# A fused layernorm, window attention and gated projection on one core: group scaling issued later, V copies on two engines, one load and the last rows rearranged

## The chip, the core and the metric

The kernel runs on one core of a Trainium2 chip. A core has a matrix engine (TensorE, PE in the profile; its weight loads are shown as PEld), a vector engine (VectorE, DVE), an activation engine (ScalarE, ACT), a general engine (GpSimd, POOL), and a queue processor (SyncE, SP) that here only issues DMAs. Each engine works through its own list of instructions in order and waits on semaphores for the others. Matmul results go to PSUM, which has eight banks of 128 x 512 fp32; everything else lies in SBUF or, outside, in DRAM. The metric is the time of one execution on the device in microseconds; lower is better.

## What is computed

```python
x  = A_x                                   # 1 x 2048 x 640, bf16
xn = (x - mean) / sqrt(var + 1e-5)
# A: attention, 32 heads of 20, causal window of 256 rows
q, k, v = split(xn @ wqkv)                 # 640 x 1920
scores = (q @ k.T) * 20 ** -0.5            # masked: 0 <= i - j < 256
o = softmax(scores) @ v
# B: gated projection
h = sigmoid(xn @ w_gate) * (xn @ w_up)     # 640 x 1536 each
return x + o @ wo + h @ w_down
```

## The kernel before

The 2048 rows are cut into four chunks `c` of 512, and a chunk into four slices `s` of 128 rows. A chunk passes these stages:

- `g_norms`: mean and variance on DVE (`bn_stats`, `bn_aggr`), `rstd` on POOL (`rstd_block`), then `xn` on DVE (`norm_block`); a DMA transpose on SP (`turn_block`) gives `xnT`. Chunk 0 is transposed on PE.
- `g_qk`: five blocks of q and five of k, each of 5 matmuls of 512 columns (`proj_block`, L297). Each block is cast to bf16 in a tile `st` (q on DVE L301, k on ACT L303), stored to a DRAM scratch (L305) and read back in another layout by `spread` (L312). The pool of `st` has five buffers; the warm-up at the start used the first one.
- `g_v`: V of each slice in two halves of 5 matmuls with 320 columns (`project_v` L323), copied to the tile `v` by `copy_v` (L330), on DVE by default.
- `g_gu`: gate and up projections, 12 blocks each of 5 matmuls (`pg` L395, `pu` L402). ACT makes `th` = tanh(pg/2) (L398, one buffer), DVE makes `h` = (th + 1) * pu (L406).
- `g_out`: for each slice, `down` accumulates 12 matmuls per half of 320 columns (L415), `outp` adds 5 matmuls with `wo` (L428), then DVE adds x (`add_half`, L433), and SP stores the rows (L448). The factor 2 of `h` is undone by the scale 0.5 there.

The attention of a chunk runs beside this in steps. A step has the score matmuls (L465, to one tile `ps` of four banks), two exponentials on ACT (L471), and maskings on POOL (L475). When the steps of a group of four heads are done, `pv` (L496) multiplies by V into the bank `acc`, and `finish_group` has DVE transpose `acc` to the tile `t1` (L506, one buffer), take the reciprocal of the sums (L508), scale the pieces (L512), and transpose a full set back to `oc` (L516). `oc` is read by the `wo` matmuls of that chunk's output.

Two things set the order. Each engine gets its instructions in the order in which the Python code issues them. The dense stages are generators in a list (`Fill`); a loop over the attention steps issues one step, and pulls dense pieces up to the share of work that belongs to it. So a dense piece of 5 to 6 matmuls is the unit between two attention steps. Before a step, `pv` of a group that ended two steps earlier is issued, with its `finish_group`.

The pool `ps_d` has three PSUM banks in turn for all dense results (pqk, pv, pg, pu, y), `acc` has one, `ps` four. At the end the `ps` banks are returned, and all four slices of the last chunk do `down` first (with the last group's `pv` after slice 1), each half in a bank of its own, then all do `outp`. The last slice stores its two halves separately, the first from ACT's queue and the second from SP's.

At the start SP issues, in this order: rows of chunk 0 and the V part of `wqkv`, the q and k parts, the first halves of `w_gate` and `w_up`, the x rows of chunk 1 (`load_x(1)`, 640 KB), and `clear` twice (zeros into the padding of the scratch, 384 KB each); then come the stores of q and k blocks as these are made.

Of the kernel before, what the change touches and what calls it, by code (L numbers as in the profile page):

```python
# [9 lines left out]
P = 128  # L10
S = 2048
D = 640
# [3 lines left out]
DC = D // P  # L16
FC = F // P
CW = 512
NCH = S // CW
SBC = CW // P  # L20
HG = 4
NG = H // HG
GH = NG // 2
VW = DH + 1
HALF = 320
# [4 lines left out]
ADD = mybir.AluOpType.add  # L30
MULT = mybir.AluOpType.mult
# [3 lines left out]
BF16 = mybir.dt.bfloat16  # L35
FP32 = mybir.dt.float32
# [75 lines left out]
def kernel(  # L112
# [11 lines left out]
    nc = tc.nc  # L124
    x2 = A_x.flatten_outer_dims()
    out2 = out.flatten_outer_dims()
# [7 lines left out]
    lnp = pool("lnp", 4)  # L134
# [11 lines left out]
    ps_a = pool("ps_a", 1, space=bass.MemoryType.PSUM)  # L146
    ps_d = pool("ps_d", 3, space=bass.MemoryType.PSUM)
# [6 lines left out]
    xc = {}  # L154

    def load_x(c):
        t = xp.tile([P, SBC, D], BF16, name="xc")
        xc[c] = t
        nc.sync.dma_start(out=t, in_=xr[:, c * SBC:(c + 1) * SBC, :])
# [5 lines left out]
    wd = const.tile([P, FC, D], BF16, name="wd")  # L165
# [33 lines left out]
            nc.sync.dma_start(out=t[k], in_=w.rearrange("(c p) f -> p c f", p=P)[:, :, k * FS:(k + 1) * FS])  # L199

    load_gu(0)
    load_x(1)
    clear("q", 0)
    clear("k", 0)

# [84 lines left out]
    def proj_block(w, c, m):  # L290


        base = 0 if w == "q" else D
        ps = ps_d.tile([P, CW], FP32, name="pqk", tag="d")
        for d in range(DC):
            wt = wqkv[:, d, base:base + D].rearrange("p (k m) -> p m k", m=DC)
            nc.tensor.matmul(ps, lhsT=wt[:, m, :], rhs=xnT[c][:, d, :],  # L297
                             start=(d == 0), stop=(d == DC - 1))
        st = stp.tile([P, CW], BF16, name="st")
        if w == "q":  # L300
            nc.vector.tensor_copy(out=st, in_=ps)  # L301
        else:
            nc.scalar.copy(out=st, in_=ps)  # L303
        dst = scratch[w, c % 2].rearrange("(h j) s -> h j s", j=32)
        nc.sync.dma_start(out=dst[:, 4 * m:4 * m + 4, :], in_=st)  # L305
# [27 lines left out]
    def proj_v(c, s, hf, copy=nc.vector.tensor_copy):  # L333
        copy_v(c, s, hf, project_v(c, s, hf), copy)
# [26 lines left out]
    def g_qk(c):  # L361
        for w in "qk":
            for m in range(DC):
                proj_block(w, c, m)
                if w == "k" and m == 1:
                    spread("q", c, 0, NG if c else 2)
                yield 5 * MM
        if c == 0:
            spread("k", c, 0, 1)
            spread("k", c, 1, 3)  # L370
            spread("q", c, 2, 4)
            spread("k", c, 3, 4)

    def g_v(c):
        for s in range(SBC):
            new_v(c, s)
            for hf in range(2):
                proj_v(c, s, hf)
            if s == 0:
                spread("k", c, 0, 2)  # L380
                spread("k", c, 2, NG)
            yield 10 * 136
# [26 lines left out]

    oc = {}  # L410

    def down(c, s, ys):
        for hf in range(2):
            for f in range(FC):
                nc.tensor.matmul(ys[hf], lhsT=ht[c, f][:, s * P:(s + 1) * P],  # L415
                                 rhs=wd[:, f, hf * HALF:(hf + 1) * HALF],
                                 start=(f == 0), stop=False)
                if f == 5:
                    yield 6 * 136
            yield 6 * 136  # L420

    def outp(c, s, ys, last=False):
        sb = c * SBC + s
        y = lnp.tile([P, D], BF16, name="xn", bufs=5)

        def wo_half(hf):
            for m in range(DC):
                nc.tensor.matmul(ys[hf], lhsT=oc[c, m][:, s * P:(s + 1) * P],  # L428
                                 rhs=wo[:, m, hf * HALF:(hf + 1) * HALF],
                                 start=False, stop=(m == DC - 1))  # L430

        def add_half(hf):
            nc.vector.scalar_tensor_tensor(  # L433
                out=y[:, hf * HALF:(hf + 1) * HALF], in0=ys[hf], scalar=0.5,
                in1=xc[c][:, s, hf * HALF:(hf + 1) * HALF], op0=MULT, op1=ADD)

        if last:
            for hf in range(2):
                wo_half(hf)
                add_half(hf)  # L440
                cut = slice(hf * HALF, (hf + 1) * HALF)
                (nc.scalar, nc.sync)[hf].dma_start(out=out2[sb * P:(sb + 1) * P, cut], in_=y[:, cut])
        else:
            wo_half(0)
            wo_half(1)
            add_half(0)
            add_half(1)
            nc.sync.dma_start(out=out2[sb * P:(sb + 1) * P, :], in_=y)  # L448
        yield 10 * 136

    def g_out(c):
        for s in range(SBC):
            ys = [ps_d.tile([P, CW], FP32, name=f"y{i}", tag="d")[:, 0:HALF] for i in range(2)]
            yield from down(c, s, ys)
            yield from outp(c, s, ys)


    def scores(c, step):
# [30 lines left out]
    def pv(c, g, parts):  # L489
        acc = ps_a.tile([P, CW], FP32, name="acc")  # L490
        flat = [(pt, *piece[1:]) for step, pt in parts for piece in step["pv"] if piece[0] == g]
        for k, (pt, r, q, n, col) in enumerate(flat):
            v = vt[c * SBC + r]
            for i in range(HG):
                h = g * HG + i
                nc.tensor.matmul(  # L496
                    acc[32 * i:32 * i + 32, q * U:(q + n) * U],
                    lhsT=v[:, h * VW:h * VW + 32], rhs=pt[:, i, col * U:(col + n) * U],
                    start=(k == 0), stop=(k == len(flat) - 1), skip_group_check=True)
        finish_group(c, g, acc)  # L500
# [3 lines left out]
    def finish_group(c, g, acc):  # L504
        t1 = np_.tile([P, 16, 32], FP32, name="t1")
        nc.vector.transpose(out=t1.rearrange("p b r -> p (b r)"), in_=acc)  # L506
        rec = np_.tile([P, 16, 1], FP32, name="rec")
        nc.vector.reciprocal(rec, t1[:, :, DH:VW])  # L508
        for m, slot, first, n in pieces_of(g):
            if slot == 0:  # L510
                on[m] = onp.tile([P, 16, 32], BF16, name="on")
            nc.vector.tensor_tensor(out=on[m][:, :, slot:slot + n], in0=t1[:, :, first:first + n],  # L512
                                    in1=rec.to_broadcast([P, 16, n]), op=MULT)
            if slot + n == 32:
                oc[c, m] = op.tile([P, CW], BF16, name="oc")
                nc.vector.transpose(out=oc[c, m], in_=on[m].rearrange("p b r -> p (b r)"))  # L516


    class Fill:
        def __init__(self):  # L520
            self.parts = []
            self.done = set()
            self.shut = set()

# [8 lines left out]
        def one(self):  # L533
            label, gen, _ = self.parts[0]
            try:
                cost = next(gen)
                self.parts[0][2] -= cost
                return cost
            except StopIteration:
                self.parts.pop(0)  # L540
                self.done.add(label)
                return 0

        def pull(self, ns):
            while ns > 0 and self.parts and self.parts[0][0] not in self.shut:
# [118 lines left out]
    for t, (c, k, step) in enumerate(todo):  # L664
        if k == 0 and c > 0:
            fill.until(f"qk{c}")
        if k == 2 and c > 0:
            fill.until(f"v{c}")
        for group in [x for x in ends if ends[x] == t - 2]:
            pv(*group, parts.pop(group))  # L670
            if group[1] == NG - 1:
                fill.shut.discard(f"out{group[0]}")
        made = (step, scores(c, step))
        for g in dict.fromkeys(piece[0] for piece in step["pv"]):
            parts.setdefault((c, g), []).append(made)
        last, label = next(x for x in cuts if t < x[0])
        credit += fill.left(label) * step["units"] / sum(x[2]["units"] for x in todo[t:last])
        credit = fill.pull(credit)
    fill.pull(10 ** 9)

    c = NCH - 1

    def run(gen):
        for _ in gen:
            pass

    banks.close()
    ps_y = pool("ps_y", 2 * (SBC - 1) - 2, space=bass.MemoryType.PSUM)
    homes = [(ps_y, "y")] * 4 + [(ps_d, "d")] * 3 + [(ps_a, "acc")]
    tiles = [lambda p=p, n=n: p.tile([P, CW], FP32, name=n)[:, 0:HALF] for p, n in homes]  # L690
    ys = [None] * SBC
    for s in range(SBC):
        ys[s] = [tiles[2 * s](), tiles[2 * s + 1]()]
        run(down(c, s, ys[s]))
        if s == 1:
            pv(c, NG - 1, parts.pop((c, NG - 1)))
    for s in range(SBC):
        run(outp(c, s, ys[s], s == SBC - 1))
# [1 line left out]
_INS = ['A_x', 'A_wqkv', 'A_wo', 'B_x', 'B_w_gate', 'B_w_up', 'B_w_down']  # L700
_OUTS = [((1, 2048, 640), 'bfloat16')]
# [25 lines left out]
```

The softmax here doesn't subtract the row's maximum and nothing guards it: scores larger than these inputs give would overflow.

## Time and profile before

| what | value |
|---|---|
| time, median of 8 runs | 320.09 us (319.18 to 321.51) |
| time of the profiled execution | 321.19 us |
| its span, first to last instruction | 319.2 us, granted clock 1.00 |
| PE busy | 307.1 us (96%), 4353 matmuls |
| PEld busy | 174.5 us (55%) |
| DVE busy | 160.3 us (50%) |
| ACT busy | 192.9 us (60%) |
| POOL busy | 177.8 us (56%) |
| DMA | 33.05 MB, mean 104 GB/s |
| V copies on DVE, L330, one | 0.49 us |
| V copies on ACT, L330, one | 0.43 us |
| acc transpose on DVE, L506, mean | 0.713 us |
| final add, L433, one | 0.49 us |

Busy shares are averages over the whole span. A matmul's end is modelled, and some matmul records are missing, so spacing is better taken from starts of blocks. In the timeline a line is: start, duration, engine, line and operation, output and inputs, shape, count, and in brackets the idle time before it with the instruction that ended it. A wait that is put down to an engine which had long finished is really for something else, often a DMA.

### The profile page before, as it was taken

What the parts mean: (1) busy time and instruction counts of PE and PEld (TensorE: products, weight loads), DVE (VectorE), ACT (ScalarE), POOL (GpSimd) and SP (SyncE); (2) the same over time, 40 slices, a digit from 0 to 9 for tenths busy, and PEclk for the clock granted to TensorE, in tenths of its full rate; (3) what the DMA queues carried; (4) which work ended last, traced back from release to release, by engine and by line L of the source; (5) the groups of instructions that cost most, each with busy time, mean ns of one, the idle gap of its engine ahead of it and who ended that gap; (6) DMA issues with size and microseconds to landing.
All of it is one profiled execution on the core that took longest, in us unless ns stands there. A gap on an engine that the chain in (4) does not pass through costs nothing.

```text
span 319.2 us, 10236 instructions
## 1 busy us (share of the span) xinstructions
PE 307.1 (96%) x4353; PEld 174.5 (55%) x4393; DVE 160.3 (50%) x324; ACT 192.9 (60%) x243; POOL 177.8 (56%) x417
## 2 busy tenths in 40 slices
PE   7899999999989999999999999999999999999996
PEld 2554444556556655644466655544456664444674
DVE  3541396665863464556753543644552544463224
ACT  4614687788655458578644457576765668778200
POOL 3000287766778637664975647466366767576300
PEclk9999999999999999999999999999999999999999
DMA  7974967926746354510046025600000010000002
GB/s 257 373 268 137 322 236 90 348 80 200 249 110 61 68 170 131 194 45 3 0 40 90 23 91 151 210 3 3 2 2 23 26 42 3 2 2 2 0 2 82
DMA packets 34428, 33.05 MB, mean 104 GB/s; under 512 B 9648, under 2 KB 33840, under 8 KB 34352
## 3 DMA queue, kind: packets, MB, share of 16 engines
q1 hardware_dynamic: 34096, 32.17, 34.6%
q8 instruction: 34, 0.56, 0.8%
q10 hardware_dynamic: 288, 0.25, 0.3%
q14 instruction: 10, 0.08, 0.1%
HBM read 21.00 MB, written 10.26 MB: 98 GB/s over the span
## 4 chain that ended last, share of the span: by engine, by line
PE 80%; DMA 6%; ACT 4%; DVE 3%; POOL 2%; issue 2%; SPq 1%; ACTq 0%; POOLq 0%
PE y L415 14%; PE pg L395 13%; PE pu L402 13%; PE pqk L297 13%; PE ps L465 7%; PE acc L496 6%; PE y L428 6%; PE pv L323 4%; ACT pT L471 3%; DMA wo_i<-in_A_wo_dram 2%; DMA xc<-in_A_x_dram 2%; PE d L415 2%; DMA sk<-st 1%; POOL pT L475 1%; DMA wo<-wo_i 1%
## 5 line engine op out<-in xcount | busy, mean ns | idle before, releaser
L475 POOL TENSOR_SCALAR_AFFINE_SELECT pT<-pT 128x256 bf16<-128x256 bf16 (+1 forms) x352 | 163.0, 497 | 119.3 <-ACT pT L471 119.2
L471 ACT ACTIVATE pT<-ps 128x1280 bf16<-128x1280 f32 (+2 forms) x152 | 147.4, 1023 | 70.2 <-PE ps L465 63.8
L406 DVE SCALAR_TENSOR_TENSOR h<-th,pu 128x512 bf16<-128x512 f32 x48 | 32.8, 684 | 58.0 <-PE pu L402 30.9
L395 PE MATMUL pg<-xnT,wg 128*128 128x512 bf16 x222 | 58.7, 380 | 1.3 <-DVE h L406 0.3
L402 PE MATMUL pu<-xnT,wu 128*128 128x512 bf16 x228 | 58.0, 380 | 1.1 <-issue 0.6
L415 PE MATMUL y<-wd,h 128*128 128x320 bf16 x336 | 49.4, 300 | 0.0
L297 PE MATMUL pqk<-xnT,wqkv 128*128 128x512 bf16 x190 | 45.7, 381 | 1.2 <-ACT st L303 0.6
L415 PEld LDWEIGHTS <-h 128*128 128x128 bf16 x384 | 36.1, 98 | 14.4 <-issue 0.2
L506 DVE STREAM_TRANSPOSE t<-acc 128x512 f32<-128x512 f32 x32 | 22.8, 713 | 33.3 <-PE acc L496 32.9
L398 ACT ACTIVATE th<-pg 128x512 f32<-128x512 f32 x48 | 28.9, 602 | 17.3 <-DVE h L406 10.0
L402 PEld LDWEIGHTS <-wu 128*128 128x128 bf16 x240 | 22.0, 98 | 25.4 <-issue 0.6
L395 PEld LDWEIGHTS <-wg 128*128 128x128 bf16 x240 | 22.0, 98 | 25.2 <-issue 0.8
L465 PE MATMUL ps<-qT,kT 20*64 20x64 bf16 (+3 forms) x2048 | 32.8, 232 | 0.7 <-ACT pT L471 0.6
L465 PEld LDWEIGHTS <-kT 20*64 20x64 bf16 x2048 | 22.2, 104 | 20.2 <-issue 16.8
L297 PEld LDWEIGHTS <-wqkv 128*128 128x128 bf16 x200 | 22.5, 119 | 18.7 <-issue 1.5
L433 DVE SCALAR_TENSOR_TENSOR xn<-y,xc 128x320 bf16<-128x320 f32 x28 | 13.6, 490 | 30.5 <-PE y L428 30.5
L496 PE MATMUL acc<-pT,v 128*32 128x128 bf16 (+2 forms) x928 | 25.7, 250 | 0.0
L323 PE MATMUL pv<-wqkv,xnT 128*128 128x320 bf16 x160 | 24.1, 300 | 1.5 <-ACT xnT L278 0.9
L496 PEld LDWEIGHTS <-v 128*32 128x32 bf16 x928 | 16.9, 97 | 15.3 <-issue 11.0
L428 PE MATMUL y<-wo,oc 128*128 128x320 bf16 x140 | 21.2, 299 | 1.2 <-DMA wo<-wo_i 1.2
L512 DVE TENSOR_TENSOR on<-t,rec 128x320 bf16<-128x320 f32 (+4 forms) x48 | 20.5, 428 | 1.1
L323 PEld LDWEIGHTS <-xnT 128*128 128x128 bf16 x160 | 14.7, 98 | 8.6 <-ACT xnT L278 1.3
(49 smaller groups left out, 151.7 us busy)
## 6 DMA issues: line engine op xcount, KB each, us to landing
qT<-sq SPq DMA_DIRECT2D x3, 1024.0 KB, 5.8
sq<-st SPq DMA_DIRECT2D x20, 128.0 KB, 2.2
sk<-st SPq DMA_DIRECT2D x20, 128.0 KB, 3.3
out_dram<-xn SPq DMA_DIRECT2D x15, 160.0 KB, 1.8
kT<-sk SPq DMA_DIRECT2D x3, 768.0 KB, 4.9
wg<-in_B_w_gate_dram SPq DMA_DIRECT2D x2, 960.0 KB, 7.2
wu<-in_B_w_up_dram SPq DMA_DIRECT2D x2, 960.0 KB
xc<-in_A_x_dram SPq DMA_DIRECT2D x3, 640.0 KB, 12.0
```

The costliest lines, as they stand in the source:

```text
L297: nc.tensor.matmul(ps, lhsT=wt[:, m, :], rhs=xnT[c][:, d, :], start=(d == 0), stop=(d == DC - 1))
L323: nc.tensor.matmul(ps[:, 0:HALF], lhsT=xnT[c][:, d, s * P:(s + 1) * P], rhs=wqkv[:, d, 2 * D + hf * HALF:2 * D + (hf + 1) * HALF], start=( ...
L395: nc.tensor.matmul(pg, lhsT=part(wg, d, f), rhs=xnT[c][:, d, :], start=(d == 0), stop=(d == DC - 1))
L398: nc.scalar.activation(out=th, in_=pg, func=TANH, scale=0.5)
L402: nc.tensor.matmul(pu, lhsT=part(wu, d, f), rhs=xnT[c][:, d, :], start=(d == 0), stop=(d == DC - 1))
L406: nc.vector.scalar_tensor_tensor(out=h, in0=th, scalar=1.0, in1=pu, op0=ADD, op1=MULT)
L415: nc.tensor.matmul(ys[hf], lhsT=ht[c, f][:, s * P:(s + 1) * P], rhs=wd[:, f, hf * HALF:(hf + 1) * HALF], start=(f == 0), stop=False)
L428: nc.tensor.matmul(ys[hf], lhsT=oc[c, m][:, s * P:(s + 1) * P], rhs=wo[:, m, hf * HALF:(hf + 1) * HALF], start=False, stop=(m == DC - 1))
L465: nc.tensor.matmul(ps[hf * U:(hf + 1) * U, i, col * U:(col + n) * U], lhsT=qk["k", kc][32 * i:32 * i + DH, g, key:key + U], rhs=qk["q", c] ...
L471: nc.scalar.activation(out=pt[:, :, to * U:(to + n) * U], in_=ps[:, :, col * U:(col + n) * U], func=EXP, scale=SCALE)
L475: nc.gpsimd.affine_select(out=out, in_=in_, pattern=[[0, HG], [sign, pattern]], compare_op=GE, fill=0.0, base=base, channel_multiplier=-sign)
L496: nc.tensor.matmul(acc[32 * i:32 * i + 32, q * U:(q + n) * U], lhsT=v[:, h * VW:h * VW + 32], rhs=pt[:, i, col * U:(col + n) * U], start=( ...
```

## The change

Four edits:

1. `load_x(1)` is taken out of the start and issued in `g_qk` of chunk 0, after the second q block, so behind two q stores and the two clears on SP's queue.
2. In `g_v` the second half of each slice is copied by `nc.scalar.copy` (ACT), the first half stays on DVE. This concerns chunks 1 to 3: 12 of 24 copies move.
3. `finish_group` issues only the transpose of `acc`. The rest (`scale_group`) is put in a list `behind`, and issued after the next dense piece that has matmuls, or before the next `pv`. The last group of the last chunk is scaled at once.
4. At the end, the last slice is cut in three column pieces, of 320, 192 and 128 columns, each with a bank of its own. `down` of the first two is issued with the rest, that of the third after all other rows, and after the first two pieces have been finished. The pieces are stored from ACT, SP and ACT.

`down`, `outp` and `g_out` are split into smaller functions (`down` takes one column range, `add_wo`, `add_x`, `store`), with the same instructions in the same order for all other slices.

```diff
@@ start
 load_gu(0)
-load_x(1)
 clear("q", 0)
 clear("k", 0)
@@ g_qk
                 proj_block(w, c, m)
+                if c == 0 and w == "q" and m == 1:
+                    load_x(1)
@@ g_v
-                proj_v(c, s, hf)
+                proj_v(c, s, hf, nc.scalar.copy if hf else nc.vector.tensor_copy)
@@ finish_group
         nc.vector.transpose(out=t1.rearrange("p b r -> p (b r)"), in_=acc)
+        if c < NCH - 1 or g < NG - 1:
+            fill.behind.append(lambda: scale_group(c, g, t1))
+        else:
+            scale_group(c, g, t1)
+
+    def scale_group(c, g, t1):
         rec = np_.tile([P, 16, 1], FP32, name="rec")
         nc.vector.reciprocal(rec, t1[:, :, DH:VW])
...
@@ Fill.one
                 cost = next(gen)
+                if cost:
+                    self.flush()
...
+        def flush(self):
+            while self.behind:
+                self.behind.pop(0)()
@@ loop over steps
         for group in [x for x in ends if ends[x] == t - 2]:
+            fill.flush()
             pv(*group, parts.pop(group))
...
@@ end
-    homes = [(ps_y, "y")] * 4 + [(ps_d, "d")] * 3 + [(ps_a, "acc")]
...
-    for s in range(SBC):
-        run(outp(c, s, ys[s], s == SBC - 1))
+    homes = [(ps_y, "y")] * 4 + [(ps_d, "d")] * 3 + [(ps_a, "acc")] + [(ps_y, "y")]
...
+        for cut in HALVES if s < SBC - 1 else HALVES[:1]:
+            ys[s, cut] = next(tiles)
+            run(down(c, s, ys[s, cut], cut))
...
+    s = SBC - 1
+    cuts = (HALVES[0], (HALF, 4 * P), (4 * P, D))
+    ys[s, cuts[1]] = next(tiles)
+    run(down(c, s, ys[s, cuts[1]], cuts[1]))
+    for k in range(s):
+        outp(c, k, [ys[k, cut] for cut in HALVES])
+    rows = new_rows()
+    for cut, queue in zip(cuts, (nc.scalar, nc.sync, nc.scalar)):
+        if cut == cuts[2]:
+            ys[s, cut] = next(tiles)
+            run(down(c, s, ys[s, cut], cut))
+        add_wo(c, s, ys[s, cut], cut)
+        add_x(c, s, ys[s, cut], cut, rows)
+        store(c, s, rows, cut, queue)
```

More of the change, by code (lines that the diff above doesn't have):

```diff
@@ L410 @@
     oc = {}
[L412 to L422, printed above, removed]
-        sb = c * SBC + s
[L424 to L449, printed above, removed]
@@ new lines, with down, add_wo @@
+    HALVES = ((0, HALF), (HALF, D))
+    def down(c, s, y, cut):
+        for f in range(FC):
+            nc.tensor.matmul(y[:, 0:cut[1] - cut[0]], lhsT=ht[c, f][:, s * P:(s + 1) * P],
+                             rhs=wd[:, f, cut[0]:cut[1]], start=(f == 0), stop=False)
+            if f % 6 == 5:
+                yield 6 * 136
+    def add_wo(c, s, y, cut):
+        for m in range(DC):
+            nc.tensor.matmul(y[:, 0:cut[1] - cut[0]], lhsT=oc[c, m][:, s * P:(s + 1) * P],
+                             rhs=wo[:, m, cut[0]:cut[1]], start=False, stop=(m == DC - 1))
@@ new lines, in add_x, with new_rows, store, outp @@
+    def add_x(c, s, y, cut, rows):
+        nc.vector.scalar_tensor_tensor(
+            out=rows[:, cut[0]:cut[1]], in0=y[:, 0:cut[1] - cut[0]], scalar=0.5,
+            in1=xc[c][:, s, cut[0]:cut[1]], op0=MULT, op1=ADD)
+    def new_rows():
+        return lnp.tile([P, D], BF16, name="xn", bufs=5)
+    def store(c, s, rows, cut=(0, D), queue=nc.sync):
+        sb = c * SBC + s
+        queue.dma_start(out=out2[sb * P:(sb + 1) * P, cut[0]:cut[1]], in_=rows[:, cut[0]:cut[1]])
+    def outp(c, s, ys):
+        rows = new_rows()
+        for y, cut in zip(ys, HALVES):
+            add_wo(c, s, y, cut)
+        for y, cut in zip(ys, HALVES):
+            add_x(c, s, y, cut, rows)
+        store(c, s, rows)
@@ L451, in g_out @@
     def g_out(c):
         for s in range(SBC):
-            ys = [ps_d.tile([P, CW], FP32, name=f"y{i}", tag="d")[:, 0:HALF] for i in range(2)]
-            yield from down(c, s, ys)
-            yield from outp(c, s, ys)
+            ys = [ps_d.tile([P, CW], FP32, name=f"y{i}", tag="d") for i in range(2)]
+            for y, cut in zip(ys, HALVES):
+                yield from down(c, s, y, cut)
+            outp(c, s, ys)
+            yield 10 * 136
     def scores(c, step):
@@ L521, in __init__ @@
             self.parts = []
+            self.behind = []
             self.done = set()
@@ L679 @@
     fill.pull(10 ** 9)
+    fill.flush()
     c = NCH - 1
@@ L688 @@
     ps_y = pool("ps_y", 2 * (SBC - 1) - 2, space=bass.MemoryType.PSUM)
-    homes = [(ps_y, "y")] * 4 + [(ps_d, "d")] * 3 + [(ps_a, "acc")]
-    tiles = [lambda p=p, n=n: p.tile([P, CW], FP32, name=n)[:, 0:HALF] for p, n in homes]
-    ys = [None] * SBC
+    homes = [(ps_y, "y")] * 4 + [(ps_d, "d")] * 3 + [(ps_a, "acc")] + [(ps_y, "y")]
+    tiles = (p.tile([P, CW], FP32, name=n) for p, n in homes)
+    ys = {}
     for s in range(SBC):
-        ys[s] = [tiles[2 * s](), tiles[2 * s + 1]()]
-        run(down(c, s, ys[s]))
+        for cut in HALVES if s < SBC - 1 else HALVES[:1]:
+            ys[s, cut] = next(tiles)
+            run(down(c, s, ys[s, cut], cut))
         if s == 1:
             pv(c, NG - 1, parts.pop((c, NG - 1)))
-    for s in range(SBC):
-        run(outp(c, s, ys[s], s == SBC - 1))
+    s = SBC - 1
[4 more added lines that the diff above has]
+        outp(c, k, [ys[k, cut] for cut in HALVES])
+    rows = new_rows()
+    for cut, queue in zip(cuts, (nc.scalar, nc.sync, nc.scalar)):
[5 more added lines that the diff above has]
+        store(c, s, rows, cut, queue)
 _INS = ['A_x', 'A_wqkv', 'A_wo', 'B_x', 'B_w_gate', 'B_w_up', 'B_w_down']
```

## The prediction

> **What bounds the kernel now.** I read the page first: TensorE (PE) is busy 307.1 of 319.2 us, so only the 12 us in which it stands still can be won. The list of PE's waits names the candidates (engine, line, releaser: total us, times, longest):
>
> ```profile
> PE y L428 <- DMA wo<-wo_i: 1.2, 1, 1.2
> PE pv L323 <- ACT xnT L278: 0.9, 1, 0.9
> PE pqk L297 <- ACT st L303: 0.6, 1, 0.6
> PE ps L465 <- ACT pT L471: 0.6, 1, 0.6
> ...
> PE pv L323 <- DVE v L330: 0.5, 1, 0.5
> PE pg L395 <- DVE h L406: 0.3, 1, 0.3
> ```
>
> Each of these happens once. The rest of the 12 us is the start before 1.25 us, and 3.1 us after the last matmul. The program is one PE queue in fixed order, and the instruction order of the changed kernel keeps PE's order up to the last rows; so a stall removed moves everything behind it forward by its size, unless a later wait is for something that does not move. The view counts a stall from a matmul's modelled end; I size them between starts (start of the block + matmuls x step; the chain of waits gives five 512-wide ones 1.08, so 0.216 a step, and twelve 320-wide ones 1.63, so 0.136), which is somewhat more.
>
> **Step 1, the x rows of chunk 1 behind two stores.** The timeline of the start, then microsecond windows (us; PE, PEld, DVE, ACT, POOL busy; clock; DMA share; GB/s):
>
> ```profile
> 17.31 4.83 SPq L305 DMA_DIRECT2D sq<-st  x5
> 24.10 1.56 ACT L303 CAST st<-pqk 128x512 bf16<-128x512 f32 x3 [6.65 <-PE pqk L297]
> 24.73 2.32 PE L297 MATMUL pqk<-xnT,wqkv 128*128 128x512 bf16 x10 [0.63 <-ACT st L303]
> ...
> 21.00:22.00 1.00, 1.00 (x7) 0.51 (x6) 0.59 (x1) 0.00 (x0) 0.00 (x0) 1.00 0.13 37
> 24.00:25.00 1.00, 0.37 (x3) 0.17 (x2) 0.00 (x0) 0.90 (x2) 0.00 (x0) 1.00 0.06 22
> ```
>
> The cast of the first k block at 24.10 is put down to PE, but PE had finished that block at about 15.3 + 30 x 0.216 = 21.8. What it really waits for is a buffer: st has 5 (one was used by the warm-up), so k block 0 reuses the buffer of q block 0 and needs that store landed. Issued at 17.31, it lands near 24.0, because up to 20 the DMA share is 1.0 with older traffic, and after that one engine of the sixteen lags (share 0.06 is one sixteenth). Ahead of it lie the 640 KB of x chunk 1: at the 375 GB/s of those windows, 1.75 us. Moved behind two stores, q block 0 is free at about 22.3; the cast ends at 22.9, and PE wants that bank at 15.31 + 40 x 0.216 = 23.95. PE's stall (24.73 - 23.95 = **0.78**) goes. Late next: q block 2, now behind x; the backlog up to it is what it was, so its buffer comes no later than before (by 25.1), and the bank that depends on it is wanted at 26.1. SP: behind x's issue stand three q stores and everything later. That issue took 2.56 us before, with the queue full; should it take this again, the q stores are issued by 22.6, still ahead of their turn. The two clears move 2.6 us forward and nothing reads them early. The spread of q waits for the last q store (about 26.0 as before), so the spreads of k gain perhaps 0.15, not 0.78. The first one is issued at 30.22 and goes through in 31 to 32 (DMA share 0.66 after 0.00); the first scores move from 33.45 to 32.7. It fits by about 0.6. x itself is first read at 39.48 by DVE, 15 us after it lands. Range of the step: -0.8 (all) to 0.
>
> **Step 2, scaling behind the next dense part.** DVE's list changes at some ten places: after the transpose of acc (0.71), the next cast, h or V copy goes first, then reciprocal, scalings and oc transpose (0.8 to 2.0 us together). No work is added. It pays only where PE stalls for it. Two such places:
>
> ```profile
> 198.82 0.72 DVE L506 STREAM_TRANSPOSE t<-acc 128x512 f32<-128x512 f32 x1 [0.29 <-PE acc L496]
> 199.07 2.21 PE L323 MATMUL pv<-wqkv,xnT 128*128 128x320 bf16 x15
> ...
> 201.25 1.90 DVE L330 CAST v<-pv 128x320 bf16<-128x320 f32 x4
> 201.78 0.84 PE L323 MATMUL pv<-wqkv,xnT 128*128 128x320 bf16 x5 [0.51 <-DVE v L330]
> ...
> 271.46 0.68 DVE L406 SCALAR_TENSOR_TENSOR h<-th,pu 128x512 bf16<-128x512 f32 x1
> 272.23 0.60 ACT L398 ACTIVATE th<-pg 128x512 f32<-128x512 f32 x1 [0.91 <-DVE h L406]
> 274.71 0.43 PE L465 MATMUL ps<-qT,kT 20*64 20x320 bf16 x28 [0.58 <-ACT pT L471]
> ```
>
> At 199 the V copy of slice 1 is ready at 199.9 but stands behind the scaling until 201.25. First, it frees its bank at 200.4; PE wants it at 199.07 + 15 x 0.136 = 201.1. Gain 201.78 - 201.1 = **0.67**. The scaling then ends at 202.1, the next DVE copy at 202.6, and its bank is wanted at 203.0. At 269 the h is ready at 270.5 and comes at 271.46; th has one buffer, so ACT's tanh and the exponentials behind it are late. First, tanh starts at 271.5 (its matmuls end), the exponentials end at 274.05, and PE arrives at 272.88 + 5 x 0.216 + 0.1 = 274.06: **0.65** gained.
>
> The third DVE stall, 0.5 us at 53, does not go: there the xn of the last block now stands between transpose and h, and its rstd leaves POOL only at 51.58 + 0.58 = 52.16. h comes at 52.65 instead of 52.71. DVE stands idle from 50.4 to 52.2 and the scaling follows later; the next h slips from 54.1 to about 54.9, which ACT, in exponentials until 55.8, does not notice: **0.05** gained. If that cover failed, it would cost 0.8. Elsewhere h, casts and copies come up to 1 us earlier or later with no PE wait nearby: 0.
>
> **Step 3, V copies.** Twelve of 24 leave DVE (12 x 0.49 = 5.9 us) for ACT (L330 on ACT at the start: 0.43 each, 5.2 us). DVE at 50% and ACT at 60% both have room; the stall this helps is the one counted above. A copy on ACT can stand behind a pair of exponentials (1.94). With three banks PE wants a copy's bank three blocks later. I laid ACT's changed order over the three V stages: copies end at 76.95, 130.1 and 201.73 where PE wants the banks at 77.48, 130.69 and 202.3: cover of 0.53 to 0.59. Cost 0 inside it; outside it, below.
>
> **Step 4, the last rows.** The tail before:
>
> ```profile
> 315.18 0.84 PE L428 MATMUL acc<-wo,oc 128*128 128x320 bf16 x5
> 316.06 0.49 DVE L433 SCALAR_TENSOR_TENSOR xn<-acc,xc 128x320 bf16<-128x320 f32 x1 [0.19 <-PE acc L428]
> 316.58 0.33 SPq L442 DMA_DIRECT2D out_dram<-xn  x1
> ...
> 11.18 0.45 PE L277 MATMUL pt<-ident,xn 128*128 128x128 bf16 x5
> ```
>
> 17 matmuls of 320 columns (17 x 0.136 = 2.31) become 17 of 192 and 17 of 128. The 128-wide ones have a near row, the transposes: 0.45 for five, of which the last runs 0.22, so 0.056 a step, each with its own weight load. 192: 0.08 to 0.083, between the two. Sum 17 x (0.082 + 0.056) = 2.35: +0.04. A rule speaks against this: the Trainium skill, TensorE: Matmul & The Clock Gate, Back-to-back issue gap, gives about 81 ns sustained for a weight load and matmul of N=128, and says that 56 under-counts it. By it the last piece costs 17 x 0.025 = 0.43 more and the tail loses. I take the row, from this kernel with loads between, and keep 0.43 for the range. The final add goes over 128 instead of 320 columns: by the scaling's rows on the same engine (L512: 0.49 for 128x320, 0.29 for 128x128) 0.20 less: -0.20. The store's rows fall to 256 bytes. The skill, DMA: Bandwidth & Descriptors, Specifications, wants 512 bytes or more; below, a read-modify-write. Packets of 640 bytes end the kernel now; with 8 per engine, even doubled times are about 0.1, against 0.1 saved if bytes count: 0. ACT issues in 0.34, SP in 0.33: 0. The added bank was row 0's, free since 312. Tail: **-0.16**, from -0.3 to +0.3.
>
> **Sum.** 0.78 + 0.67 + 0.65 + 0.05 + 0.16 = 2.3 us. The profiled execution has a span of 319.2 and a time of 321.19, so 316.9 and 318.9 for it; it lies 1.1 above the median 320.09, from which the forecast is **317.8**.
>
> **Rivals.** (a) *Half of it*: one gain is taken back. The wo weights reach PE by DMA at 92.27 with PE waiting 1.2; if they were bound to DMA traffic alone, the 0.8 won earlier would be waited away there. For it: their queue on SP waited 3.5 us for k stores. Against: those stores follow ACT's casts of PE's blocks, so the chain moves along. Or the k casts wait on q block 2 behind x. Either way 1.5 is left: 318.6. (b) *Nothing*: the order moves, other waits close the gaps: 320.1. (c) *Slower, ACT in the V stages*: if V copies fall over 0.55 behind my layout, they stand behind the next exponentials as well; PE then waits 1.94 - 0.55 = 1.4 per copy, one per V stage: +4.2 - 2.3 = 322.0. For it: ACT is 7 to 8 tenths busy there. Against: each pair of exponentials waited 0.2 to 1.9 for PE's scores in those stages, so ACT runs behind nothing.
>
> **Numbers.** Forecast 0.60, (a) 0.20, (b) 0.10, (c) 0.10. No change is what lies within 0.3% (1 us). Faster: forecast and most of (a), 0.77; same: (b) and the rest, 0.13; slower 0.10. The likeliest has 317.1 to 318.5 (tail 0.4, start 0.3); the range, with (a) and a little of (b), is 316.7 to 319.7.
>
> **What would show it.** Right: no PE wait for st, v or the exponentials at 274; the wait for wo near 1.2 and for h near 0.3 still there; final add 0.29; last pieces 0.056 a step. Wrong: a V copy on ACT named as PE's releaser; k casts still starting at 24; the final matmuls at 0.08.

## The result, and the profile after

| | before | after |
|---|---|---|
| time, median | 319.84 us (57 runs, 319.10 to 322.35) | 317.34 us (20 runs, 316.63 to 319.68) |
| ratio, 95% interval | | 0.9925 (0.991 to 0.994) |
| the profiled execution: time, span | 321.19, 319.2 us | 316.96, 315.0 us |

The change makes the kernel faster by 0.75%, 2.4 us by this ratio (its interval: 1.9 to 2.9) and 2.5 between the medians. The forecast was 317.8. The two profiled executions lie 4.2 us apart, more than the medians; what the extra is made of is worked out below.

The page after, engines' busy time (us, share of the span, instructions):

```profile
PE 306.4 (97%) x4370; PEld 175.3 (56%) x4410; DVE 154.3 (49%) x313; ACT 198.1 (63%) x255; POOL 178.9 (57%) x417
```

DVE gave up 6.0 us and ACT took 5.2: the 12 V copies. PE's work is what it was; it lies closer together. Its list of waits after:

```profile
PE pwarm L240 <- DVE st L169: 1.3, 1, 1.3
PE y L424 <- DMA wo<-wo_i: 1.1, 1, 1.1
PE pu L403 <- issue: 0.6, 4, 0.2
PE pt L276 <- DVE xn L268: 0.6, 1, 0.6
PE pu L403 <- PE ps L463: 0.2, 1, 0.2
```

Of the six lines shown of before, only that for `wo` is left (1.2 to 1.1). The waits for `st`, the exponentials, `v`, and also `h`, which was to stay, are gone from the list, and so is the 0.9 for `xnT` at the start, which the change does not touch.

The timeline after, at the k casts, in the V stage near 197, at the exponentials near 271, and at the end:

```profile
20.78 0.58 ACT L302 CAST st<-pqk 128x512 bf16<-128x512 f32 x1 [4.53 <-PE pqk L296]
23.02 0.59 ACT L302 CAST st<-pqk 128x512 bf16<-128x512 f32 x1 [0.57 <-DMA sq<-st]
...
196.50 2.89 PE L322 MATMUL pv<-wqkv,xnT 128*128 128x320 bf16 x20
197.39 0.49 DVE L329 CAST v<-pv 128x320 bf16<-128x320 f32 x1 [0.42 <-PE pv L322]
198.59 0.44 ACT L329 CAST v<-pv 128x320 bf16<-128x320 f32 x1
199.68 1.53 PE L322 MATMUL pv<-wqkv,xnT 128*128 128x320 bf16 x10
...
268.30 0.60 ACT L399 ACTIVATE th<-pg 128x512 f32<-128x512 f32 x1 [0.22 <-PE pg L396]
270.82 0.43 PE L463 MATMUL ps<-qT,kT 20*64 20x320 bf16 x28
...
311.06 0.83 PE L417 MATMUL y<-wd,h 128*128 128x128 bf16 x12
311.74 0.44 PE L424 MATMUL y<-wo,oc 128*128 128x128 bf16 x5
312.21 0.29 DVE L428 SCALAR_TENSOR_TENSOR xn<-y,xc 128x128 bf16<-128x128 f32 x1 [0.59 <-PE y L424]
```

The k casts keep PE's rhythm. Twenty V matmuls run in one piece where fifteen were followed by a wait of 0.51. The scores at 270.82 carry no bracket: the exponentials came in time. The last add takes 0.29, as the scaling's row said it would.

**Where the extra between the two profiles comes from.** At the start, ACT waits for the rows of slice 3 (before, then after):

```profile
8.85 0.74 ACT L575 ACTIVATE xn<-xc 128x640 bf16<-128x640 bf16 x1 [2.78 <-DMA xc<-in_A_x_dram]
```

```profile
7.55 0.74 ACT L586 ACTIVATE xn<-xc 128x640 bf16<-128x640 bf16 x1 [1.38 <-DMA xc<-in_A_x_dram]
```

The load was issued at the same time in both, and nothing ahead of it differs. It landed 1.3 us apart, and the first q block followed: at 15.31 before, at 14.10 after. Of the profiled executions below, those whose start is that of before had that q block at 15.48 and 15.57 (e1, e3), and between 14.22 and 14.59 in the other six (e4 to e7, e11, e12); e2, with the x load moved, had it at 15.46. So 1.2 of the 4.2 us come from when that one transfer landed, and do not follow the change. The rest, between starts of PE's blocks: 0.78 at `st`, 0.41 at `h`, 0.67 at `v`, 0.65 at the exponentials, 0.25 at the end, and 0.17 less at `wo`, which adds up to the difference.

### The profile page after: what moved, and what is told of

Its sections match the earlier page's. It is cut to its first block, busy times and chain, and to the rows that moved or that the text cites. A ratio compares the mean times of both kernels' runs of the same rounds, so it can differ in the third digit from the quotient of the medians.

```text
span 315.0 us, 10274 instructions
## 1 busy us (share of the span) xinstructions
PE 306.4 (97%) x4370; PEld 175.3 (56%) x4410; DVE 154.3 (49%) x313; ACT 198.1 (63%) x255; POOL 178.9 (57%) x417
## 4 chain that ended last, share of the span: by engine, by line
PE 88%; DMA 5%; ACT 3%; issue 2%; SPq 1%; DVE 0%; ACTq 0%
PE pu L403 16%; PE pg L396 16%; PE y L417 14%; PE pqk L296 13%; PE ps L463 8%; PE acc L494 7%; PE y L424 6%; PE pv L322 5%; DMA wo_i<-in_A_wo_dram 2%; PE d L417 2%; DMA sk<-st 1%; ACT pT L469 1%; DMA wo<-wo_i 1%; DMA xc<-in_A_x_dram 1%; SPq L220 1%
## 5 line engine op out<-in xcount | busy, mean ns | idle before, releaser
L473 POOL TENSOR_SCALAR_AFFINE_SELECT pT<-pT 128x256 bf16<-128x256 bf16 (+1 forms) x352 | 164.8, 502 | 114.4 <-ACT pT L469 114.2
L417 PE MATMUL y<-wd,h 128*128 128x320 bf16 (+1 forms) x348 | 50.2, 297 | 0.0
L428 DVE SCALAR_TENSOR_TENSOR xn<-y,xc 128x320 bf16<-128x320 f32 (+1 forms) x29 | 13.9, 483 | 30.5 <-PE y L424 30.5
L424 PE MATMUL y<-wo,oc 128*128 128x320 bf16 (+1 forms) x145 | 21.6, 297 | 1.1 <-DMA wo<-wo_i 1.1
L300 DVE CAST st<-pqk 128x512 bf16<-128x512 f32 x20 | 13.7, 690 | 12.2 <-PE pqk L296 11.4
```

The lines of the kernel that those rows point to most:

```text
L417: nc.tensor.matmul(y[:, 0:cut[1] - cut[0]], lhsT=ht[c, f][:, s * P:(s + 1) * P], rhs=wd[:, f, cut[0]:cut[1]], start=(f == 0), stop=False)
L424: nc.tensor.matmul(y[:, 0:cut[1] - cut[0]], lhsT=oc[c, m][:, s * P:(s + 1) * P], rhs=wo[:, m, cut[0]:cut[1]], start=False, stop=(m == DC - 1))
L473: nc.gpsimd.affine_select(out=out, in_=in_, pattern=[[0, HG], [sign, pattern]], compare_op=GE, fill=0.0, base=base, channel_multiplier=-sign)
```

## The experiments

My theory then: the scaling moved back is worth about 1.8 us by three stalls, V's copies help only the one at 201, the tail is worth 0.2, and the x load next to nothing, since the stall at `st` may have been one execution's. Its rival is the prediction's own sum, with 0.78 for the x load. Kernels e2 to e4 and e6 do one part each, e5 does two and e7 undoes one; e1 is the kernel before as it stands, to see how far equal kernels differ. Each ratio is to the kernel before as it ran beside that kernel (medians 319.62 with e1 to e4, 319.71 with e5 to e8, 319.49 with e9 to e12).

| kernel | median, us | ratio to before (95%) | span of its profile |
|---|---|---|---|
| e1, before again | 319.60 | 1.0000 (0.9988 to 1.0011) | 318.6 |
| e2, x load alone | 319.49 | 1.0001 (0.9987 to 1.0015) | 318.5 |
| e3, V copies alone | 319.73 | 0.9999 (0.9986 to 1.0012) | 318.5 |
| e4, scaling alone | 318.37 | 0.9964 (0.9949 to 0.9978) | 315.8 |
| e5, scaling and V copies | 317.87 | 0.9942 (0.9920 to 0.9964) | 315.6 |
| e6, tail alone | 319.24 | 0.9990 (0.9973 to 1.0006) | 317.1 |
| e7, changed kernel, x load put back | 317.31 | 0.9927 (0.9905 to 0.9950) | 315.5 |
| e8, changed kernel, `wo` earlier | 317.15 | 0.9919 (0.9899 to 0.9940) | 315.3 |
| e9, changed kernel, `wo` first | 315.79 | 0.9878 (0.9848 to 0.9907) | 313.9 |
| e10, changed kernel, all V copies on ACT | 318.77 | 0.9968 (0.9954 to 0.9982) | 316.6 |
| e11, scaling of the second group alone | one run, 319.60 | | 317.6 |
| e12, scaling of the first two groups | one run, 319.32 | | 317.4 |

**Before again.** No edit.

> The kernel before, unchanged, for a second profile. Theory 1: the 1.2 us by which the first q block started earlier after the change (14.1 instead of 15.3) belong to one execution, not to the change: here the wait of V's matmuls for the transposed rows at about 9 us is of another size than 0.9, while the waits for st (0.6), wo (1.2), v (0.5), the exponentials (0.6) and h (0.3) are there again; ratio 1.000. Theory 2: the change itself shortened the start: the wait of 0.9 at 9 us is there again, within 0.1.

Equal kernels agree within 0.1%. The wait for `xnT` is 0.9 again, which by the expectation spoke for the change as what shortened the start; the early starts of e4 to e7, e11 and e12, and the late one of e2, speak against that. And its profile shows no wait of PE for `st`, which the first theory had expected again:

```profile
15.48 9.88 PE L297 MATMUL pqk<-xnT,wqkv 128*128 128x512 bf16 x45
22.82 1.07 ACT L303 CAST st<-pqk 128x512 bf16<-128x512 f32 x2 [5.19 <-DMA sq<-st]
```

Here the profile itself names the store as what ends the cast's wait, which the prediction had only inferred. But the cast comes at 22.82, not at 24.10, and PE, with three banks, goes on without a gap.

**The x load alone.**

```diff
 load_gu(0)
-load_x(1)
 clear("q", 0)
@@ g_qk
                 proj_block(w, c, m)
+                if c == 0 and w == "q" and m == 1:
+                    load_x(1)
```

> The load of x for chunk 1 is moved, nothing else. Theory 1 (buffer of q block 0 behind 640 KB of x): the cast of k block 0 starts as soon as its matmuls end, PE's wait for st is gone, 0.8 us less, ratio 0.9975, and the later waits for h, wo, v and the exponentials stay at 0.3, 1.2, 0.5 and 0.6. Rival (the wo transfer does not move along): its wait grows from 1.2 to 2.0 and the time stays, ratio 1.000.

**The changed kernel with the x load put back.** The same edit in reverse, from the changed kernel.

> The changed kernel with the load of x for chunk 1 put back to the start. Theory 1 (the load's place seldom costs PE anything: k's first cast came late in all four traces with it in front, but PE waited for it in one): 0 to 0.3 more than the changed kernel, ratio to before 0.9925 to 0.9935. Rival (it is worth the 0.8 of the first profile, and the run of it alone hid this in some other wait): ratio 0.995. The k cast waits for the store of q block 0 here in any case, to about 22.2 or later.

Both say that this part gives nothing: at most 0.4 us by the interval of e2, and e7 stands where the changed kernel stands. Of e2's expectation neither side came true: there is no wait for `st`, the one for `wo` stays at 1.1, and the time stays as well. From the first q block to the first gate block is ten blocks, 50 x 0.216 = 10.8 us if PE never waits. With the x load in front it took 11.58 in the first profile of before, 11.10 in e11, 10.97 in e12, and 10.79 or 10.80 in the other six; with it behind, 10.79 or 10.80 in all five. So there is a stall to remove in three executions of nine, 0.14 on the mean over them ((0.78 + 0.31 + 0.17) / 9). The load does what it was moved for; casts of k start earlier (e2):

```profile
22.14 0.59 ACT L302 CAST st<-pqk 128x512 bf16<-128x512 f32 x1 [4.53 <-PE pqk L296]
24.82 1.14 ACT L302 CAST st<-pqk 128x512 bf16<-128x512 f32 x2 [1.02 <-DMA sq<-st]
```

The first cast now follows PE, and the third waits for the store behind x, as foreseen for 25.1. PE waits for neither.

**V copies alone; scaling alone; both.**

```diff
-                proj_v(c, s, hf)
+                proj_v(c, s, hf, nc.scalar.copy if hf else nc.vector.tensor_copy)
```

> Half of the V copies on ACT, nothing else. Theory 1 (the stall of 0.67 at 201 is DVE's scaling standing before a V copy, and copies on ACT are covered): with fewer copies on DVE the bank that PE wants at 201 is still slice 1's first half, whose copy stays on DVE behind the scaling, so the stall stays, ratio 1.000. Rival 1 (halving alone cures it): wait for v gone, ratio 0.998. Rival 2 (ACT late behind exponentials): a V copy on ACT named as PE's releaser, ratio over 1.003.

The second has the hunks of `finish_group`, `Fill.one`, `flush` and the loop over steps as in the change, nothing else.

> Deferred scaling, nothing else. Theory 1: the waits for h at 53 (0.5), and for the exponentials at 274 (0.65) go, as does that for v at 201 for the first copy, though all eight V copies are on DVE, so that one of them may be late again; 1.2 to 1.8 us less, ratio 0.995. The one at 53 goes because POOL's four rstd are done about 0.35 earlier, counted from the same matmul, when DVE's scaling does not run beside them. Rival (as the prediction had it): POOL's rstd stay where they were and the wait for h at 53 stays at 0.3, ratio 0.996.

> Deferred scaling and half of the V copies on ACT. Theory: with the scaling alone PE still waited 0.35 at the V stage of chunk 3 for a V copy on DVE; with the second halves on ACT that rest goes too, so 0.35 less than the scaling alone (0.9964): ratio 0.995 to 0.9955, and no wait for v in the trace. Rival: the halving is worth nothing beside the deferral, ratio 0.9964. Rival 2 (ACT late behind exponentials): a V copy on ACT as PE's releaser, ratio 0.998 or more.

Alone, the V copies do nothing: PE's wait for `v` at 201 stays 0.5, since the scaling still stands before the one DVE copy that is late. Alone, the scaling is worth 1.15 us (0.7 to 1.6), nearer to the rival's 0.996 than to the 0.995 of the theory, but the wait for `h` is off the list, as only the theory had it. Of the stall at `v` a rest stays. The timeline of e4:

```profile
197.64 0.49 DVE L330 CAST v<-pv 128x320 bf16<-128x320 f32 x1 [0.42 <-PE pv L323]
198.32 0.49 DVE L330 CAST v<-pv 128x320 bf16<-128x320 f32 x1 [0.18 <-PE pv L323]
198.73 0.24 DVE L514 RECIPROCAL rec<-t 128x16 f32<-128x16 f32 x1
...
199.90 0.61 DVE L518 TENSOR_TENSOR on<-t,rec 128x256 bf16<-128x256 f32 x1
...
200.43 1.91 DVE L330 CAST v<-pv 128x320 bf16<-128x320 f32 x4
200.97 0.84 PE L323 MATMUL pv<-wqkv,xnT 128*128 128x320 bf16 x5 [0.18 <-DVE v L330]
```

The copy that was late in before (at 197.64 here) is in time, and so is the next, but the four after them stand behind the deferred scaling in their turn. With half of them on ACT (e5) that rest goes as well, and the pair is at 0.9942, 1.85 us. So the V copies are worth a good third of a microsecond by the stall (0.35 between starts), and only together with the scaling. The ratios of e4 and e5 lie 0.7 us apart, but their intervals overlap, so the clock does not size it.

**The tail alone.** The last hunk of the change, with the split of `down` and `outp` that it needs.

> The last rows in three pieces, nothing else. Theory: final add 0.29 instead of 0.49, the store of 256-byte rows lands no later than that of 640-byte rows, 17 pieces of 128 columns at 0.056 each: 0.25 less, ratio 0.9992, not told apart from 1 by the clock but seen in the trace from the last down block to the end. Rival 1 (weight loads bind narrow matmuls, 0.081 a step): the last 17 take 1.4 instead of 0.95. Rival 2 (a penalty for rows under 512 bytes): the last store lands later after its issue than the 1.30 of before.

Both rivals are the rules that the prediction took from the Trainium skill. By time this part is not told apart from nothing: 0.9990, the interval reaching 1.0006. By the rows it is as in the changed kernel:

```profile
313.17 0.83 PE L416 MATMUL y<-wd,h 128*128 128x128 bf16 x12
314.32 0.29 DVE L427 SCALAR_TENSOR_TENSOR xn<-y,xc 128x128 bf16<-128x128 f32 x1 [0.59 <-PE y L423]
```

Twelve matmuls of 128 columns take 0.83, of which the last runs 0.22: eleven steps of 0.056. From the end of the last matmul to the end of the span it takes 2.83 to 2.85 in all six executions that have this tail, and 3.11 to 3.13 in all eight that have the old one.

**Why the wait for `h` at 53 went.** The prediction left it. The rows of before there:

```profile
53.43 1.24 PE L395 MATMUL pg<-xnT,wg 128*128 128x512 bf16 x5 [0.34 <-DVE h L406]
...
44.17 0.51 DVE L512 TENSOR_TENSOR on<-t,rec 128x320 bf16<-128x320 f32 x1
44.31 0.46 POOL L263 TENSOR_SCALAR rstd<-mv 128x1 f32<-128x1 f32 x1
...
50.70 0.71 DVE L512 TENSOR_TENSOR on<-t,rec 128x192 bf16<-128x192 f32 x1
51.18 0.31 POOL L263 TENSOR_SCALAR rstd<-mv 128x1 f32<-128x1 f32 x1
...
52.25 0.54 DVE L269 TENSOR_SCALAR xn<-xc,mv,rstd 128x640 bf16<-128x640 bf16 x1
52.71 0.67 DVE L406 SCALAR_TENSOR_TENSOR h<-th,pu 128x512 bf16<-128x512 f32 x1
```

and after:

```profile
42.31 0.23 POOL L262 TENSOR_SCALAR rstd<-mv 128x1 f32<-128x1 f32 x1
...
48.95 0.21 POOL L262 TENSOR_SCALAR rstd<-mv 128x1 f32<-128x1 f32 x1
...
49.86 0.52 DVE L268 TENSOR_SCALAR xn<-xc,mv,rstd 128x640 bf16<-128x640 bf16 x1 [1.71 <-POOL rstd L263]
50.30 0.67 DVE L407 SCALAR_TENSOR_TENSOR h<-th,pu 128x512 bf16<-128x512 f32 x1
```

The small add on POOL takes 0.46 and 0.31 where DVE's scaling runs beside it, and 0.21 to 0.23 where it does not. At 44 it ends at 44.77, just after the scaling's 44.68, and at 51 at 51.49, just after 51.41. POOL goes from maskings to adds with hardly a gap in this stretch, so its fourth `rstd`, for which DVE's `xn` and then `h` wait, is 0.33 later in before (0.23 + 0.10). To test this, e11 defers only the second group's scaling (the one ahead of the late `h`), and e12 the first group's as well (the one beside the add at 44).

```diff
-        if c < NCH - 1 or g < NG - 1:
+        if c == 0 and g == 1:
```

> The kernel before, with the scaling deferred for one group alone: the second of chunk 0, which stood before the h that PE waits for at 53. Theory (POOL's rstd chain sets that h, and the scaling of the first group, beside it on DVE, holds up one rstd by 0.24): the first rstd add still takes 0.46, h comes 0.15 earlier than before and PE still waits for it, 0.2 to 0.4 of 0.5. Rival (the order on DVE alone decides): the wait is gone.

```diff
-        if c < NCH - 1 or g < NG - 1:
+        if c == 0 and g < 2:
```

> The kernel before, with the scaling deferred for the first two groups of chunk 0. Theory (POOL's chain): the first rstd add takes 0.23, POOL's fourth rstd ends 0.35 earlier counted from the maskings before, and PE's wait for h at 53 is gone, while those for v and for the exponentials stay at 0.5 and 0.6. Rival (as the prediction had it): the first rstd add stays at 0.46 and a wait of 0.3 stays.

The measure is the time from the `h` near 40 to this `h`, which does not depend on the start. The last column is what the list of waits shows; the one before it is the time between the starts of PE's block before the wait and of the block that waits, about 1.09 if PE does not wait:

| kernel | first add on POOL | fourth add | from `h` to `h` | between PE's starts | PE waits for `h` |
|---|---|---|---|---|---|
| before; e1; e2; e3 | 0.46 | 0.31 to 0.32 | 11.19; 11.21; 11.21; 11.22 | 1.59 to 1.62 | 0.3 to 0.4 |
| e11 | 0.46 | 0.22 | 11.01 | 1.09 | none, see below |
| e12 | 0.23 | 0.22 | 10.79 | 1.18 | none |
| after | 0.23 | 0.21 | 10.78 | 1.18 | none |

So what PE won here is 0.41, and 0.1 of the stall of 0.5 is still there, too short for the list. Deferring the second group gives 0.18 to 0.21, deferring the first as well another 0.22, which is the first add's 0.23: the chain through POOL is shown. The times of these two are single runs and say nothing by themselves. In e11 PE's wait cannot be read, because in that execution PE had itself been held up before:

```profile
42.32 1.25 PE L402 MATMUL pu<-xnT,wu 128*128 128x512 bf16 x5 [0.35 <-DMA wu<-in_B_w_up_dram]
42.84 0.46 POOL L263 TENSOR_SCALAR rstd<-mv 128x1 f32<-128x1 f32 x1
```

e12 is the clean one: no wait for `h` in the list, with those for `v` (0.5) and the exponentials (0.6) still there.

A section of the Trainium skill speaks of this: SBUF — State Buffer, SBUF: two separate sides, has DVE and GpSimd share one pair of ports, held for a whole instruction; a DVE operation with two SBUF inputs, like this scaling, and a GpSimd one that reads SBUF block each other. The traces agree in part: of the 168 such adds in the fourteen of them, 46 begin during a scaling; these take 0.31 to 0.48 and end 0.08 to 0.09 after it. Not every pair behaves so: in the changed kernel the power on POOL (L263 at 43.47, 0.57) overlaps the scaling at 43.62 (0.49), and both keep their lengths. What no run here shows is the port as such.

**All V copies on ACT.**

```diff
-                proj_v(c, s, hf, nc.scalar.copy if hf else nc.vector.tensor_copy)
+                proj_v(c, s, hf, nc.scalar.copy)
```

> The changed kernel with all 24 V copies of chunks 1 to 3 on ACT. Theory (a copy behind a pair of exponentials is 1.9 late, and the cover is three banks): PE waits for ACT's V copies 0.6 to 1 in each V stage, together 2 to 3: ratio to before 0.998 to 1.002. Rival (ACT has room for all): ratio 0.9925 and no such wait.

```profile
PE pv L322 <- ACT v L329: 1.5, 4, 0.4
```

This is rival (c) brought about, at less than its size: four waits of PE behind exponentials on ACT (0.54, 0.49, 0.60 and 0.54 between starts, where 0.6 to 1 in each V stage were expected), and 1.4 us lost against the changed kernel. Two of the four come before 80 us, and the wait for `wo` at 90 is gone in turn: PE came later, and the weights were there. In the changed kernel the ACT copy at 198.59 ends at 199.03, and PE takes its bank again at 199.68, as the timeline after shows: a cover of 0.65, where the prediction had counted 0.57. Twelve copies fit in such a cover where 24 do not.

**The wait that stayed: `wo`.** `turn_wo` copies `w_o` to DRAM in another order, and `load_wo` reads it back. In the changed kernel that is late (timeline after):

```profile
77.50 2.81 SPq L220 DMA_DIRECT2D wo_i<-in_A_wo_dram  x4
82.99 3.64 SPq L225 DMA_DIRECT2D wo<-wo_i  x4
89.69 1.52 PE L424 MATMUL y<-wo,oc 128*128 128x320 bf16 x10 [1.06 <-DMA wo<-wo_i]
```

Two places are tried for the copy: behind the load of `w_down`, and right after `load_rest()`. In both the reading back follows V of chunk 1.

```diff
@@ e8
     fill.add("wd", later(load_wd), 0)
+    fill.add("wo_i", later(turn_wo), 0)
     fill.add("qk1", g_qk(1), 50 * MM)
     fill.add("v1", g_v(1), 40 * 136)
-    fill.add("wo_i", later(turn_wo), 0)
+    fill.add("wo", later(load_wo), 0)
...
-    fill.add("wo", later(load_wo), 0)
@@ e9
 load_rest()
+turn_wo()
...
     fill.add("v1", g_v(1), 40 * 136)
-    fill.add("wo_i", later(turn_wo), 0)
+    fill.add("wo", later(load_wo), 0)
...
-    fill.add("wo", later(load_wo), 0)
```

> The changed kernel, with the turning of wo through DRAM issued behind the load of w_down, before the q blocks of chunk 1, and its read back where the turning was. Theory: the wait for wo (1.1 to 1.4) goes, as the data is there by 85: ratio to before 0.9885 to 0.9890. Rival: the 25.6 KB pieces and the w_down load delay q's stores of chunk 1, whose buffers k's casts need; PE waits for st near 65 to 75 instead, and the spread of q and k is later: ratio 0.992 or more.

> The changed kernel, with the turning of wo through DRAM issued at the end of the first loads (about 37 us, SP idle until 44), and its read back where the turning was. Theory (behind the w_down load it held up q's stores, earlier it meets nothing that is waited for): the wait for wo goes and no wait for the exponentials at 68 comes; 1.1 to 1.4 less than the changed kernel, ratio to before 0.9885 to 0.989. Rival: its 0.8 MB come before the transposed rows and the second weight halves have landed, so PE waits for those at about 41 or 57: ratio 0.992.

In e8 the wait for `wo` goes, and another of about the same size comes in its place, 20 us earlier:

```profile
52.85 3.93 SPq L220 DMA_DIRECT2D wo_i<-in_A_wo_dram  x4
...
67.27 0.58 ACT L302 CAST st<-pqk 128x512 bf16<-128x512 f32 x1 [2.37 <-DVE on L516]
67.75 1.95 ACT L469 ACTIVATE pT<-ps 128x1280 bf16<-128x1280 f32 x2
...
69.75 0.42 PE L463 MATMUL ps<-qT,kT 20*64 20x320 bf16 x16 [1.39 <-ACT pT L469]
```

The copy is now just ahead of chunk 1's q stores, which are issued from 58.9 on in both kernels. From issue to landing these take up to 8.3 us, against at most 3.7 in the changed kernel (of those whose landing is on record); the first lands at 67.17. ACT's first k cast starts 0.1 after that: as at 24 in before, it needs the buffer of the first q block, though its wait is put down to DVE. In the changed kernel it started at 65.14. The exponentials behind it on ACT are then late (67.75, against 66.28), and PE's next scores wait for them. This is the rival that was named, save that PE waits at the scores and not for `st`. So the time barely moves: 0.9919. In e9 the copy is issued at 37.58, when no q or k store stands behind it for 20 us. PE's waits in e9, all that the list has:

```profile
PE pwarm L240 <- DVE st L169: 1.3, 1, 1.3
PE pt L276 <- DVE xn L268: 0.5, 1, 0.5
```

e9 takes 315.79 us (315.61 to 316.17), 0.9878 of before: faster than both kernels, 1.5 us below the changed one, of which the wait accounts for 1.1 to 1.2; where the rest comes from is not shown. More buffers for `st`, the other way to free the k casts, were not tried.

## Why the prediction was right, and where its steps were not

The sum was right: 2.3 us expected, 2.4 measured. Its parts were not all so; two errors point in opposite directions, and that the sum came so near is luck.

- **Step 1 (0.78) failed.** The reading was right: the cast waits for a buffer, and moving x frees it. The size was wrong: PE's 0.78 belonged to that one execution; six of the nine with x in front ran the stage in its bare 10.8. What the prediction missed is that this stall was part of why the profiled execution lay 1.1 us above the median. It took the 1.1 off as a constant, and then won the 0.78 from the median as well: counted twice. The late x rows of the start are another part: e1's profiled execution had these without the stall, and lay 1.0 above its median and 0.6 below that of before. The reason given for the late store was too simple as well: in the windows left out between the two shown, the DMA share was 0.60 and 0.25 (22 to 24 us), so more than one engine was still at work there.
- **Step 2, "the third DVE stall, 0.5 us at 53, does not go: 0.05", failed the other way.** The order on DVE was laid out rightly, and `xn` does stand before `h`. But POOL's `rstd` was held at its old time, and it moves: of the 0.41 by which `h` gains, 0.33 come from two small adds that no longer run beside the scaling. To PE it was worth 0.41 (between starts) instead of 0.05. This error makes up for half of that of step 1 (0.78 counted, 0.14 there on the mean), so the total alone would have confirmed both.
- **Step 2, `v` at 201 and the exponentials at 274 (0.67 and 0.65): right** in place and size; both waits are gone. Scaling and V copies together measure 1.85 (e5), and what was won at `h`, `v` and the exponentials adds up to 1.7.
- **Step 3, V copies at 0: right as a cost**, since no copy on ACT is named as PE's releaser in the changed kernel. As a benefit it was under-read. The 0.67 at 201 had been put down to the scaling alone; it needed both edits, 0.35 of it the copies.
- **Step 4 (0.16): right in kind, measured 0.25.** From the last matmul's end to the end of the span it was 3.13 and is 2.83: 0.20 from the add, and 0.1 that is left for the smaller store. The price of the extra matmuls was 0.05 (the stage from the last `down` is 7.27 after 7.22). The step was 0.056, so the loss of 0.43 by the skill's 81 ns did not come. Nor did one for rows under 512 bytes: in the records of the DMA queues (medians in before and after) a packet of 640 bytes took 32 to 35 ns, one of 384 bytes 22, one of 256 bytes 18. For the skill's rule on 512 bytes that shows only that these stores have no such cost.
- **`wo`, "near 1.2 and still there": right** (1.1). It did not grow by what was won ahead of it (0.41 at `h`, 0.78 at `st` in these two profiles), so rival (a) did not happen: its loads follow PE's chain, as argued. Over all executions that have this wait the list gives it 0.9 to 1.4, with no order by what was won ahead. Rival (c) took all 24 copies to happen (e10).
- **The count of PE's 12 us** at the head left out 2.7 us of the same list (`pwarm` 1.3, `pt` 0.6, `pu` 0.6 and 0.2). The change touches none of them, so the forecast does not rest on it.

The parts as they were found (0.14, 0.41, 0.67, 0.65 and 0.25) add up to 2.1, inside the 1.9 to 2.9 of the measured interval.

## What to carry to other kernels

A stall that is seen in one profiled execution may be what makes that execution slow; before it is counted against a median, see whether a second execution has it too. When instructions are reordered on one engine, look at what ran beside them on the others. With the deferred scaling, of the 1.7 us that it won together with the V copies, 0.33 came through two small adds on POOL. And a transfer that is late for its reader is moved to where nothing urgent stands behind it on its queue, not merely earlier: the same copy gained next to nothing at 53 us (0.2) and 1.5 us at 38.

## What had not been expected of the hardware

- A one-column add on POOL takes 0.21 to 0.23, beside DVE's `bn_stats`, `h` or transposes as well as alone, and 0.31 to 0.48 where it begins during a scaling (0.46 for the first add at 42 to 44 in before, e1, e2, e3, e6 and e11). The scaling reads two tiles in SBUF, but that is not needed: ten adds that begin during an `xn`, which reads one tile and two columns, take 0.28 to 0.35 and end 0.07 to 0.08 after it.
- It goes the other way, too: a scaling of 128x320 takes 0.49 with POOL idle, and 0.69 to 0.98 at 75.11, 162.08 and 262.85 in before, where it begins as a masking does or in its first half. At 247.54, near the end of one, it keeps 0.49.
- The same first loads, issued at the same time, give the rows of slice 3 between 7.3 and 9.1 us after the start (ten of fourteen profiled executions by 8.13, four at 8.85 to 9.11), and the whole kernel follows: e1 to e3 had the late start and lay 0.75 to 1.0 above their medians, e6 the early one and 319.06 against 319.24. Those three ran on one chip with e4, which was early; e5 to e12, on two others, were all early. Whether it is chance or the chip is open.
